# The high part of the gelu of two joint chunks: cast on ScalarE instead of VectorE

## The chip, the cores and the metric

The kernel runs on one core of a Trainium2 chip. The metric is the device time of one execution in microseconds (us); lower is better. Times are medians over runs. The profile comes from one execution of the same program that was taken by the hardware profiler.

## What is computed

Attention with a sliding window and a few global keys (8 heads of 64, 4 batches of 768 rows, a bias that falls with distance), and behind it a two-layer network with an exact gelu. The second half is what the change touches:

```python
def _moe_ref(x, w_in, w_out):        # x: 3072 x 512, w_in: 512 x 2048, w_out: 2048 x 512
    h = x @ w_in
    inv_sqrt2 = np.float32(1.0 / np.sqrt(2.0))
    g = 0.5 * h * (1.0 + erf(h * inv_sqrt2))
    return (g @ w_out).astype(np.float32)

def reference(**kwargs):
    ...
    attn_out = _attn_ref(**attn_kwargs)
    B, H, S, D = attn_out.shape
    x = np.ascontiguousarray(attn_out.transpose(0, 2, 1, 3)).reshape(B * S, H * D)
    return _moe_ref(x=x, **moe_kwargs)
```

## The kernel before

The 3072 rows are cut into 12 chunks of 256 rows, and the hidden width of 2048 into 8 slices of 256. A step is one chunk with one slice: hidden layer (`m1`), gelu (`gelu`), output layer (`m2`). The list STEPS puts the steps in order: step 0 and steps 4 to 18 are the first two chunks with all slices, slice by slice; from step 19 on each later chunk goes through its eight slices.

Products are made in float16 with two parts for each operand: a high part and a low part that holds what the high part left out, so that every product is three matmuls (high with high, high with low, low with high).

The first two chunks are treated jointly from the third slice on (steps 7 to 18, slices 2 to 7): a step then takes one half of a slice for the rows of both chunks, in matmuls of 512 columns (L560), and its output products are those of L698. The 12 gelus of these steps are the ones that the change concerns.

`gelu` works on one 128x512 tile: ScalarE applies Gelu to the hidden layer in PSUM and writes it to SBUF in float32 (gr, L683), VectorE casts it, scaled, to the float16 high part (gh, L684), and VectorE takes the low part (gl, `lo_dve`, L202). Chunks 7 to 11 go another way (`gelu7`), in which ScalarE casts the high parts with activations of kind Copy (L607, L608).

While the first two chunks run, the weights are decoded: each slice comes as four blocks of 64-bit words by DMA on SP's queue (L212); ScalarE converts the low words (L238), VectorE puts the number together in three instructions (L244, L247, L249), ScalarE casts the high part (L259, Copy), and VectorE takes the low part (L202). A word block's buffer is free for the next transfer when its number has been put together.

The attention of the third chunk on (chunk 2 and later) runs beside this: scores on TensorE (L376), masking and maxima on VectorE (L388), exponentials with sums on ScalarE (L419), an addition and a reciprocal of the sums on VectorE (L428, L431), normalization on GpSimd (L437; on VectorE for the first two chunks), transposes on TensorE (L449) with copies on ScalarE (L454), and the products with the values (L488), from which ScalarE casts the high part of x (L539) and VectorE takes the low part (L201).

Exponentials and gelus use different activation tables; a switch shows as ACT_TABLE_LOAD. `table` fixes the order of exponentials and gelus among themselves. Otherwise the order of instructions on each engine is not written out: a planner follows the program's order as a priority and simulates the times, and every engine then takes its queue strictly in that order. `last_dve` (L685) holds the low part of the last gelu; work with low urgency (checks, part of the weight work) is put behind it by `behind`.

Of the kernel before, what the change touches and what calls it, by code (L numbers as in the profile page):

```python
# [13 lines left out]
AF = mybir.ActivationFunctionType  # L14
ALU = mybir.AluOpType
# [30 lines left out]
STEPS = [(c, s) for s in range(NST) for c in range(2)]  # L46
# [11 lines left out]
CAT = 2  # L58
# [4 lines left out]
GS = 2.0 ** 6  # L63
# [42 lines left out]
class Fast:  # L106
# [568 lines left out]
    def gelu(self, t):  # L675
        nc = self.nc
        if STEPS[t][0] >= SEVEN:
            return self.gelu7(t)
        hp = self.h.pop(t)
        gh = self.gp.tile([P, 2, CT], F16, name=f"gh{t}", tag="gh")  # L680
        gl = self.gp.tile([P, 2, CT], F16, name=f"gl{t}", tag="gl")
        gr = self.gp.tile([P, 2, CT], F32, name=f"gr{t}", tag="gr")
        self.table(nc.scalar.activation(out=gr, in_=hp, func=AF.Gelu, scale=1.0 / (WS * XS)))  # L683
        nc.vector.tensor_scalar(out=gh, in0=gr, scalar1=GS, scalar2=None, op0=ALU.mult)  # L684
        self.last_dve = self.lo_dve(gl, gr, gh, GS).ins  # L685
        self.g[t] = (gh, gl)

# [373 lines left out]
```

## Time and profile before

| | |
|---|---|
| median of 3 runs | 639.75 us (638.47 to 641.1) |
| the profiled execution | 639.78 us, of which 638.0 us are the profile's span |
| TensorE matmul busy | 616.9 us (97%) |
| VectorE busy | 485.0 us (76%) |
| ScalarE busy | 387.4 us (61%) |
| GpSimd busy | 83.0 us (13%) |

The profile's times count from the start of the span. PE is TensorE, PEld its weight loads, DVE VectorE, ACT ScalarE, POOL GpSimd, SP the engine that issues most DMAs. A busy time of matmuls is modelled at its end, so neighbouring matmuls overlap in the timeline. Waits are read from semaphore events: the instruction named behind "<-" is the one that came last.

### The profile page before, as it was taken

Reading aid. Unit: us, or ns where it says so; the run is one execution under the profiler, and the core shown is the slowest. Engines: PE = TensorE matmul, PEld = TensorE weight load, DVE = VectorE, ACT = ScalarE, POOL = GpSimd, SP = SyncE. Lnnn points to the kernel's source line nnn. Section 1 sums busy time; section 2 is a strip of 40 time slices with the busy share of each in tenths; the row PEclk is TensorE's granted clock in tenths of the full one; section 3 lists DMA queues with packets and bytes.
Section 4 is the critical chain, followed back from the end, with each engine's and each line's share of the span. In section 5 each row is a group of like instructions: output and inputs, shape, how many; then the busy total and the mean of one; then the engine's idle time right before and its main releaser. Section 6 shows DMA issues by size and latency. Waiting matters only on the chain.

```text
span 638.0 us, 16200 instructions
## 1 busy us (share of the span) xinstructions
PE 616.9 (97%) x6360; PEld 484.2 (76%) x6360; DVE 485.0 (76%) x1482; ACT 387.4 (61%) x891; POOL 83.0 (13%) x175
## 2 busy tenths in 40 slices
PE   7988999999999998999999999999999999999995
PEld 5555544457667887888898888888888888888884
DVE  8979999955777887857867866866856766755875
ACT  3777577754647657657567567576577477574331
POOL 3000006220203112022012022021012021020000
PEclk9988999999999999999999999999999999999999
DMA  8948825304442425143164064043064062000001
GB/s 264 271 167 238 269 96 199 116 1 149 135 131 76 124 64 154 40 145 116 37 173 133 35 174 134 35 150 117 35 174 135 34 174 68 35 1 2 34 2 38
DMA packets 66196, 71.38 MB, mean 112 GB/s; under 512 B 32705, under 2 KB 49345, under 8 KB 66113
## 3 DMA queue, kind: packets, MB, share of 16 engines
q1 hardware_dynamic: 61664, 62.93, 33.0%
q10 hardware_dynamic: 4448, 7.34, 3.2%
q8 instruction: 52, 0.85, 0.6%
q14 instruction: 32, 0.25, 0.1%
HBM read 63.97 MB, written 6.29 MB: 110 GB/s over the span
## 4 chain that ended last, share of the span: by engine, by line
PE 66%; DVE 20%; ACT 8%; issue 3%; DMA 1%; POOL 1%; SPq 0%; POOLq 0%; DVEq 0%; ACTq 0%
PE h L566 27%; PE seven L632 22%; PE av L488 4%; PE s L376 4%; PE t L449 4%; ACT n L419 4%; PE acc L698 2%; PE h L560 2%; DVE ss L606 2%; DVE sf L589 2%; DVE wb L247 1%; DVE wb L249 1%; DVE gl L202 1%; DVE sb L586 1%; DVE wb L244 1%
## 5 line engine op out<-in xcount | busy, mean ns | idle before, releaser
L566 PE MATMUL h<-x,winh 128*128 128x256 f16 x1344 | 227.5, 274 | 4.4 <-DVE mn L388 2.8
L566 PE MATMUL h<-x,winl 128*128 128x256 f16 x672 | 184.2, 274 | 0.0
L566 PEld LDWEIGHTS <-winh 128*128 128x128 f16 x1344 | 128.8, 98 | 24.6 <-DVE mn L388 4.6
L437 POOL TENSOR_SCALAR n<-n,su 128x192 f32<-128x192 f32 (+1 forms) x160 | 77.8, 508 | 483.3 <-DVE su L431 349.1
L601 ACT ACTIVATE gr<-h 128x512 f32<-128x512 f32 x72 | 43.0, 597 | 66.9 <-PE h L566 48.8
L608 ACT ACTIVATE sh<-ss 128x512 f16<-128x512 f32 x72 | 45.4, 630 | 59.6 <-DVE ss L606 59.6
L606 DVE TENSOR_TENSOR ss<-gr 128x128 f32<-128x128 f32 x144 | 37.1, 298 | 55.9 <-ACT gr L601 55.9
L632 PE MATMUL seven<-sw,sh 128*128 128x256 f16 x432 | 74.8, 273 | 0.0
L566 PEld LDWEIGHTS <-winl 128*128 128x128 f16 x672 | 66.0, 98 | 8.4 <-issue 0.5
L419 ACT ACTIVATE n<-n,mn 128x192 f32<-128x192 f32 (+1 forms) x144 | 62.1, 432 | 5.5 <-DVE mn L388 5.4
L632 PEld LDWEIGHTS <-sh 128*128 128x128 f16 x576 | 56.3, 98 | 6.5
L632 PE MATMUL seven<-sw,sl 128*128 128x256 f16 x216 | 58.9, 273 | 0.0
L388 DVE CUSTOM_DVE_ANT_0 n<-s,pens 128x192 f32<-128x192 f32 (+1 forms) x192 | 55.1, 340 | 4.2 <-PE s L376 3.8
L202 DVE SCALAR_TENSOR_TENSOR sl<-ss,sh 128x512 f16<-128x512 f32 x72 | 49.6, 689 | 10.5 <-ACT sh L608 10.5
L202 DVE SCALAR_TENSOR_TENSOR gl<-gr,gh 128x384 f16<-128x384 f32 (+1 forms) x96 | 56.4, 588 | 0.6
L449 PE MATMUL t<-ident,n 128*128 128x128 f32 x288 | 48.0, 277 | 3.2 <-DVE n L437 2.2
L454 ACT COPY pt<-t 128x384 f32<-128x384 f32 x96 | 44.6, 472 | 10.3 <-PE t L449 10.1
L632 PEld LDWEIGHTS <-gh 128*128 128x128 f16 x432 | 41.0, 98 | 9.0 <-issue 4.8
L488 PEld LDWEIGHTS av<-pt,vr 64*64 64x64 f32 (+1 forms) x1312 | 35.9, 135 | 11.8 <-issue 8.3
L376 PE MATMUL s<-kr,qr 64*64 64x192 f32 (+2 forms) x752 | 43.1, 328 | 1.5 <-DMA kr<-kT 1.5
L488 PE MATMUL av<-pt,vr 64*64 64x64 f32 (+2 forms) x1312 | 42.7, 251 | 2.0 <-ACT pt L454 2.0
L449 PEld LDWEIGHTS t<-ident,n 128*128 128x128 f32 x288 | 34.7, 142 | 10.8 <-DVE n L437 2.1
(138 smaller groups left out, 1124.0 us busy)
## 6 DMA issues: line engine op xcount, KB each, us to landing
w<-w SPq DMA_DIRECT2D x32, 512.0 KB, 6.0
c<-w SPq DMA_DIRECT2D x32, 512.0 KB, 4.3
out<-o ACTq DMA_DIRECT2D x23, 256.0 KB, 2.0
qr<-qT SPq DMA_DIRECT2D x11, 512.0 KB, 4.2
vr<-v SPq DMA_DIRECT2D x22, 256.0 KB, 4.4
kr<-kT SPq DMA_DIRECT2D x16, 320.0 KB, 5.5
vr<-v SPq DMA_DIRECT2D x19, 192.0 KB, 3.0
kr<-kT SPq DMA_DIRECT2D x36, 64.0 KB, 3.5
```

Of the source, the lines that this page charges most:

```text
L202: return self.nc.vector.scalar_tensor_tensor(out=out, in0=in_, scalar=scale, in1=hi, op0=ALU.mult, op1=ALU.subtract)
L376: ins = nc.tensor.matmul(out, lhsT=lhs, rhs=rhs, start=True, stop=True).ins
L388: ins = nc.vector.tensor_tensor_reduce(out=nn[:, j * NK:j * NK + n], in0=sp[hh][:, j, 0:n], in1=self.pens[:, 2 * p + hh, o:o + n], scale=- ...
L419: self.table(nc.scalar.activation(out=nn, in_=nn, func=AF.Exp, bias=mn[:, i:i + 1], scale=-1.0, accum_out=su[:, i:i + 1]))
L437: ins = eng.tensor_scalar(out=nn, in0=nn, scalar1=su[:, i:i + 1], scalar2=0.0, op0=ALU.mult, op1=ALU.add)
L449: self.last_t = nc.tensor.transpose(tp[:, i, :], nn[:, o:o + P], self.ident).ins
L454: ins = nc.scalar.copy(pt, tp).ins
L488: ins = nc.tensor.matmul(out, lhsT=lhs, rhs=rhs, start=start, stop=stop, skip_group_check=True).ins
L566: ins = nc.tensor.matmul(hp[:, f, :], lhsT=w[:, d, fs], rhs=x[:, d, e, :], start=n == 0, stop=n == 3 * NP - 1).ins
L606: self.last_sum = nc.vector.tensor_tensor(out=ss[:, o], in0=x, in1=y, op=op).ins
L608: self.last_table = nc.scalar.activation(out=sh, in_=ss, func=AF.Copy, scale=GS).ins
L632: ins = nc.tensor.matmul(out, lhsT=g, rhs=w, start=s == 0 and name in ("P1", "P4", "P6", "P3") and i == 0, stop=s >= NST - 4 and i == 2, s ...
```

## The change

In steps of the first two chunks from the third slice on, the high part of the gelu is made by an activation of kind Copy on ScalarE, with the same scale, instead of the multiplication on VectorE. The other gelus of `gelu`, and all that reads gh, stay as they are.

```diff
@@ -681,7 +681,10 @@
         gl = self.gp.tile([P, 2, CT], F16, name=f"gl{t}", tag="gl")
         gr = self.gp.tile([P, 2, CT], F32, name=f"gr{t}", tag="gr")
         self.table(nc.scalar.activation(out=gr, in_=hp, func=AF.Gelu, scale=1.0 / (WS * XS)))
-        nc.vector.tensor_scalar(out=gh, in0=gr, scalar1=GS, scalar2=None, op0=ALU.mult)
+        if STEPS[t][0] < CAT and STEPS[t][1] > 1:
+            nc.scalar.activation(out=gh, in_=gr, func=AF.Copy, scale=GS)
+        else:
+            nc.vector.tensor_scalar(out=gh, in0=gr, scalar1=GS, scalar2=None, op0=ALU.mult)
         self.last_dve = self.lo_dve(gl, gr, gh, GS).ins
         self.g[t] = (gh, gl)
```

## Rows read from the trace of the kernel before

**Rows 1.** The page, busy time of each engine over the span.
```profile
PE 616.9 (97%) x6360; PEld 484.2 (76%) x6360; DVE 485.0 (76%) x1482; ACT 387.4 (61%) x891; POOL 83.0 (13%) x175
```

**Rows 2.** Windows: start:end, length, busy us of each engine, clock, DMA share, GB/s.
```profile
66.00:150.00 84.00, 82.93 (x554) 41.09 (x552) 72.44 (x182) 55.24 (x124) 17.68 (x24) 1.00 0.40 130
74.00:99.00 25.00, 25.00 (x141) 11.37 (x140) 24.84 (x63) 18.29 (x40) 2.56 (x2) 1.00 0.41 140
99.00:126.00 27.00, 25.93 (x185) 12.45 (x184) 26.70 (x65) 19.13 (x45) 9.43 (x12) 1.00 0.51 167
126.00:150.00 24.00, 24.00 (x188) 13.14 (x187) 12.91 (x40) 13.84 (x34) 5.70 (x12) 1.00 0.09 29
```

**Rows 3.** TensorE's waits, 60 to 155 us: us in total, times, longest.
```profile
PE t L449 <- POOL n L437: 0.8, 1, 0.8
PE h L560 <- DVE x L201: 0.3, 1, 0.3
```

**Rows 4.** TensorE's waits, 205 to 246 us.
```profile
PE h L566 <- DVE mn L388: 2.8, 2, 2.2
```

**Rows 5.** Single lines of the kernel: ns min/median/max, first and last start, forms.
```profile
L684 DVE TENSOR_SCALAR gh<-gr x24: 407/421/573, 41.4 to 197.1; 128x512 f16<-128x512 f32 x24
...
L608 ACT ACTIVATE sh<-ss x72: 625/630/632, 204.6 to 627.8; 128x512 f16<-128x512 f32 x72
```

**Rows 6.** Timeline of VectorE: start, us, engine line operation out<-in.
```profile
90.93 0.41 DVE L684 TENSOR_SCALAR gh<-gr 128x512 f16<-128x512 f32 x1
91.26 0.67 DVE L249 CUSTOM_DVE_ANT_0 wb<-w,wb 128x1024 uint16<-128x1024 uint16 x1
...
94.19 0.15 DVE L428 TENSOR_SCALAR su<-su 128x4 f32<-128x4 f32 x1
...
96.07 0.16 DVE L431 RECIPROCAL su<-su 128x4 f32<-128x4 f32 x1
```

**Rows 7.** The chain of waits in order of time: start, us, what.
```profile
99.35 2.20 POOL n L437 x2
...
101.60 0.44 PE t L449 x2
...
147.06 2.59 PE acc L698 x12
```

**Rows 8.** Timeline of GpSimd, with the idle time before and its releaser.
```profile
96.44 2.93 POOL L437 TENSOR_SCALAR n<-n,su 128x192 f32<-128x192 f32 x2 [90.47 <-DVE su L431]
```

**Rows 9.** Timeline of ScalarE.
```profile
73.80 0.57 ACT L683 ACTIVATE gr<-h 128x512 f32<-128x512 f32 x1
74.28 0.61 ACT L259 ACTIVATE winh<-wb 128x512 f16<-128x512 f32 x1
74.80 0.61 ACT L259 ACTIVATE wouth<-wb 128x512 f16<-128x512 f32 x1
...
88.97 0.60 ACT L683 ACTIVATE gr<-h 128x512 f32<-128x512 f32 x1 [0.40 <-PE h L560]
89.58 1.28 ACT L419 ACT_TABLE_LOAD   x1
...
92.55 0.19 ACT L419 ACTIVATION_READ_ACCUMULATOR n<-n,nmax 128x1 f32 x1
...
114.63 0.60 ACT L683 ACTIVATE gr<-h 128x512 f32<-128x512 f32 x1 [1.77 <-PE h L560]
...
121.36 0.68 ACT L238 ACTIVATE w<-w 128x512 int32<-128x512 uint32 x1 [1.32 <-DMA w<-w]
...
145.59 0.60 ACT L683 ACTIVATE gr<-h 128x512 f32<-128x512 f32 x1
```

**Rows 10.** Timeline of TensorE, first output product of steps 7, 10 and 14.
```profile
79.16 0.38 PE L698 MATMUL acc<-wouth,gh 128*128 128x512 f16 x1
...
94.80 0.38 PE L698 MATMUL acc<-wouth,gh 128*128 128x512 f16 x1
...
119.62 0.39 PE L698 MATMUL acc<-wouth,gh 128*128 128x512 f16 x1
```

## The prediction

> **What bounds the kernel now.** I read the page first. TensorE is busy for 616.9 of 638.0 us [rows 1], so all idle time of TensorE together is 21 us, and only what lies near the change can move. The new casts belong to steps 7 to 18, and the table by windows puts them: between 66 and 150 us TensorE is busy 82.93 of 84.00 us at a granted clock of 1.00, and in 74 to 99 us 25.00 of 25.00 [rows 2]. Busy time is modelled, so I also looked at the pace: twelve 512-column products take 2.59 us [rows 7], 0.22 us each, and that is their distance in the whole stretch. What the stretch has to give is therefore 84.00 - 82.93 = 1.07 us.
>
> VectorE is full there as well: 24.84 of 25.00 us in 74 to 99 and 26.70 of 27.00 in 99 to 126, and it falls to 12.91 of 24.00 after 126 [rows 2]. The chain of waits runs for long parts over VectorE for that reason. It must not be read as "every us taken from VectorE is a us of the kernel", since TensorE is full beside it. The list of TensorE's waits decides: between 66 and 150 us it holds two, 0.8 us of a transpose on GpSimd's normalization and 0.3 us of a hidden-layer product on VectorE's low part of x [rows 3]. These two are the whole 1.07. Later, between 205 and 246 us, there is 2.8 us more, on the masked maxima [rows 4].
>
> **The change part by part.** Removed: 12 casts from VectorE (two chunks, slices 2 to 7). One lasts 0.421 us (median of 24) [rows 5], but the next instruction starts earlier than its end: 90.93 to 91.26 is 0.33 us [rows 6]. So VectorE gets back 12 x 0.33 = 4.0 us, of which eight casts (steps 7 to 14), 2.6 us, lie in its full stretch. The other four lie where it idles for 11.1 of 24.00 us [rows 2].
>
> What those 2.6 us reach is the 0.8 us wait. Going back from the transpose at 101.60, the chain shows two GpSimd operations from 99.35 [rows 7]. They are the last two of four that GpSimd does in one go from 96.44 on, the first two in 2.93 us [rows 8], and the reciprocal on VectorE that releases the first starts at 96.07, 1.88 us after the addition of its sums at 94.19 [rows 6]. The last of these sums is read out on ScalarE at 92.55, ending at 92.74 [rows 9]. So the addition stood in VectorE's queue for 94.19 - 92.74 = 1.45 us after its input was there. Four of the removed casts (the last at 90.93) are ahead of it, and they are worth 4 x 0.33 = 1.3 us. The reciprocal and GpSimd can begin up to 1.3 us earlier, and the transpose too. That is more than the 0.76 us that TensorE stands idle. Against this stands the cast of step 10, now on ScalarE: if it is put ahead of the table load at 89.58 [rows 9], the sums come about 0.52 us later, at 93.26, and the lead is 94.19 - 93.26 = 0.9 us instead of 1.3, still more than 0.76. Gain: 0.76 us. Bounds: 0 (the planner puts other VectorE work into the gap) and 0.76; I take the upper one, since even the smaller lead exceeds the wait.
>
> The 0.3 us wait: VectorE's low part of x follows the cast on ScalarE, which stood behind the conversion of a weight word at 121.36, itself idle for 1.32 us on a transfer [rows 9]. The word's buffer is freed by VectorE, so the transfer may come earlier by up to 2.6 us. Or the chain may grow by the cast of step 14, 0.52 us, on ScalarE ahead of the exponentials that follow the gelu of 114.63. Bounds: 0.27 gained and 0.52 lost, and as 1.32 us of idle time on ScalarE lies between that cast and the place, I take 0.
>
> Added: 12 activations of kind Copy on ScalarE. The nearest row is the same cast of the same size in the later chunks, 0.630 us [rows 5]; successors follow after 0.52 us (74.28 to 74.80) [rows 9]. That is 12 x 0.52 = 6.2 us of ScalarE's queue. Between 74 and 99 us it is busy 18.29 of 25.00 us, then 19.13 of 27.00 and 13.84 of 24.00 [rows 2]; four casts, 2.1 us, come to each, and all three have room for it. No table load is added: the weight cast at 74.28 is a Copy too and follows the gelu of 73.80 directly, with no load between [rows 9].
>
> The way from gelu to its low part: ScalarE can start the cast 0.5 us after the gelu's start and be done 0.63 us later, so 1.13 us after that start. TensorE wants the first of them at 79.16 (gelu at 73.80), the fourth at 94.80 (gelu at 88.97), the eighth at 119.62 (gelu at 114.63) [rows 9, 10]. These leave 4.2, 4.7 and 3.9 us. The tightest is the last: gelu at 145.59 [rows 9], ready at 146.72, wanted at 147.06 [rows 7], a slack of 0.34 us. Cost: nothing, hidden by the matmuls ahead of each; if the cover of the last one is gone, it costs the excess, at most about 0.5 us (one ScalarE instruction put ahead of it).
>
> The added queueing: behind each cast stand exponentials, weight casts, copies of the transposed probabilities and, at the end, casts of x. One place later is 0.52 us for each. In 126 to 150 us ScalarE idles 10 us, so this is absorbed; from the table load at 89.58 on, exponentials stand in a row, and that place I counted above. No DMA moves with the cast; SP's weight transfers wait for VectorE and can only come earlier by the 2.6 us.
>
> After 150 us the chain goes on over gelu, VectorE and ScalarE in turn, with each step released by the one before, so I expect 0.76 us to be kept. Sum: 639.78 - 0.76 = 639.0 us, made against the profiled execution's 639.78, which is beside the median of 639.75.
>
> A rule that speaks against this change: the Trainium skill, page "ScalarE: Activation LUTs", section "Rules for kernel authors", says that multiplications go to VectorE and not to ScalarE, as VectorE is up to about three times as fast per element in bf16. The rows here show the same direction, at a smaller ratio (0.630 against 0.421 us). By that rule the change should lose, as the third rival below works out from the rows.
>
> **The rivals.** First, nothing happens: TensorE is full, the planner (which orders every queue from its own estimate of times, and whose new order no trace shows) fills the gaps of VectorE with weight work, and the reciprocal stays late. For it: VectorE has no idle time before 126 us, so there is always work waiting. Against: the weight work is finite. Time: 639.8.
>
> Second, slower, by a cast that is queued behind a waiting instruction on ScalarE. An engine takes its queue in order; the place is behind the gelu of 114.63, where a table load, exponentials and weight casts follow. If the cast of step 14 is put behind the word conversion that waited until 121.36 for its transfer [rows 9], it starts at 121.36 + 0.52 = 121.9 and ends at 122.5, while TensorE wants it at 119.62 [rows 10]: 2.9 us lost. It decides from the point at which the cast starts later than 119.62 - 0.63 = 119.0. One such case gives 639.0 + 2.9 = 641.9. A second one (step 10 has a table load and the exponentials behind it as well), priced alike for want of a nearer row, makes 644.8. Against it: the cast's input is there 0.5 us after the gelu's start, and a planner that follows readiness would place it at once.
>
> Third, the slower engine counts in full: 12 x (0.630 - 0.421) = 2.5 us if every cast stood on the path, so 642.3. Against it: the 3.9 to 4.7 us of slack at three of the steps above.
>
> Fourth, more than forecast: a new order also removes the 2.8 us of waits at 205 to 246 us [rows 4]. All of both stretches is 1.07 + 2.8 = 3.9 us, so 635.9. Against it: VectorE's work there (sums for the later chunks) isn't touched.
>
> **How the numbers follow.** The forecast (a gain of 0.3 to 1.8 us) gets 0.42; nothing (within 0.3) 0.17; the second rival 0.24, of it 0.13 for two misplaced casts or more; the third 0.04; the fourth, wholly or in part, 0.13. The second gets that much because the new order can't be seen, and an order made from estimated times can be wrong in more than one place. About 0.5%, 3.2 us, is what a measurement can tell from no change, so the bounds are 636.6 and 643.0. Faster by more takes nearly all of the fourth: 0.10. Slower by more takes two misplaced casts and a little of the third: 0.14. Same: 0.76. The range goes from 635.5 (the fourth, and 0.4 for the spread of a measurement) to 642.5 (one misplaced cast or the third, with as much); two misplaced casts are left out.
>
> **What would show it.** In the profile after, 12 casts of 0.63 us on ScalarE and 12 fewer of the 24 on VectorE; GpSimd's first normalization starting about 1 us before 96.44; no wait of a transpose on GpSimd near 101; TensorE idle in 66 to 150 us falling from 1.07 to about 0.3 us. Wrong would be: TensorE waiting for the high part of a gelu on ScalarE (second rival), or a changed idle time after 150 us that outweighs 0.8 us.

## The result and the profile after

The kernel became slower: 645.99 us (median of 9 runs) against 640.92 us (median of 9), a ratio of 1.0081 with a 95% interval of 1.0061 to 1.0101. That is about 5 us against a forecast gain of 0.8 us, and above the end of the range, 642.5.

The page of the profile after has the busy times that the edit must give, and they explain nothing. VectorE falls by 4.2 us and ScalarE rises by 6.4 us, as worked out; TensorE's busy time rises by 4.5 us [rows 1], with the same 6360 matmuls. The three lines are the busy times, TensorE's slices and the granted clock, each digit a fortieth of the span:

```profile
PE 621.4 (96%) x6360; PEld 486.0 (75%) x6360; DVE 480.8 (75%) x1470; ACT 393.8 (61%) x903; POOL 77.8 (12%) x175
...
PE   8987999899999998999999999999999999999995
...
PEclk9898999899999999999999999999999999999999
```

The eighth slice (113 to 129 us) shows both parts of the loss: TensorE is less busy there, and its clock is lower. The table by windows, which answers [rows 2], puts it in 99 to 150 us (start:end, length, then busy us of TensorE, its weight loads, VectorE, ScalarE, GpSimd, granted clock, DMA share, GB/s):

```profile
66.00:150.00 84.00, 81.06 (x487) 38.89 (x485) 66.35 (x167) 58.59 (x129) 12.18 (x23) 0.96 0.38 123
...
99.00:126.00 27.00, 24.06 (x173) 11.75 (x172) 24.28 (x57) 20.14 (x41) 4.15 (x8) 0.94 0.47 163
126.00:150.00 24.00, 24.00 (x134) 11.58 (x133) 9.90 (x41) 15.32 (x39) 5.60 (x13) 0.93 0.03 5
```

In 126 to 150 us TensorE is busy without a pause both times, but it does 134 matmuls where it did 188 [rows 2], some of that because it is later in its work, some because of the clock. TensorE's waits between 60 and 150 us, which answer [rows 3], show where TensorE loses time. The wait on GpSimd is gone, as forecast, the short one on x too, and one that was not there has come:

```profile
PE acc L701 <- ACT gh L685: 2.8, 1, 2.8
PE acc L716 <- DVE gl L202: 1.0, 1, 1.0
```

L685 is the new cast, L701 the output products of the joint steps; the other wait, at 62 us, is in both kernels. ScalarE's queue shows which step it is (timeline: start, us, line, operation, and in brackets the idle time before with what ended it):

```profile
115.93 0.68 ACT L238 ACTIVATE w<-w 128x512 int32<-128x512 uint32 x1
118.69 0.71 ACT L238 ACTIVATE w<-w 128x512 int32<-128x512 uint32 x1 [2.08 <-DMA w<-w]
119.31 0.57 ACT L683 ACTIVATE gr<-h 128x512 f32<-128x512 f32 x1
119.90 1.28 ACT L419 ACT_TABLE_LOAD   x1
...
122.52 0.44 ACT L419 ACTIVATE n<-n,nmax 128x192 f32<-128x192 f32 x1
122.87 0.18 ACT L419 ACTIVATION_READ_ACCUMULATOR n<-n,nmax 128x1 f32 x1
122.96 0.61 ACT L685 ACTIVATE gh<-gr 128x512 f16<-128x512 f32 x1
```

This is step 14. The word conversion (L238, the last block of the last slice) waits 2.08 us for its transfer, the gelu stands behind it, and behind the gelu come a table load and four exponentials before the cast gets its turn. In the kernel before, the same word stood behind the gelu and the exponentials [rows 9]. What TensorE did meanwhile:

```profile
119.88 0.92 PE L376 MATMUL s<-kr,qr 64*64 64x192 f32 x16
123.63 0.61 PE L701 MATMUL acc<-wouth,gh 128*128 128x512 f16 x1 [2.82 <-ACT gh L685]
```

It stood for 2.82 us, and then ran at half the clock. In the windows from 120 us on, the clock is the third column from the end:

```profile
120.80:121.60 0.80, 0.01 (x1) 0.00 (x0) 0.56 (x1) 0.79 (x3) 0.00 (x0) 1.00 0.00 0
121.60:122.40 0.80, 0.00 (x0) 0.00 (x0) 0.00 (x0) 0.80 (x5) 0.00 (x0) 1.00 0.37 31
122.40:123.20 0.80, 0.00 (x0) 0.00 (x0) 0.12 (x2) 0.80 (x5) 0.00 (x0) 0.66 0.76 216
...
126.00:127.00 1.00, 1.00 (x3) 0.30 (x2) 0.89 (x8) 0.91 (x5) 0.61 (x2) 0.50 0.46 80
...
129.00:129.50 0.50, 0.50 (x2) 0.15 (x1) 0.50 (x2) 0.49 (x1) 0.50 (x1) 0.51 0.00 0
129.50:130.00 0.50, 0.50 (x4) 0.23 (x3) 0.29 (x1) 0.50 (x1) 0.50 (x2) 1.00 0.17 33
```

The clock stays at its upper level (2.4 GHz) for the first part of the wait, falls to 0.50 (1.2 GHz) within it and is back at 129.5 us. The chain of waits gives the price: the twelve output products of step 14 take 5.30 us, where twelve at full clock take 2.59 us [rows 7].

```profile
118.69 0.71 ACT w L238
119.40 0.47 ACT gr L683
...
123.05 0.53 ACT gh L685
123.58 0.05 issue
123.63 5.30 PE acc L701 x12
```

The profiles of these kernels differ by up to 1.9 us in their first 60 us, where all do the same work, and again near 245 us, where the clock falls in some and not in others. To compare single profiles I therefore take one distance in each: from the output product that waits 0.97 us at about 62 us (the work ahead of it is that of the kernel before in every run) to the gelu of step 19, the first of the third chunk. Before:

```profile
62.28 0.39 PE L713 MATMUL acc<-wouth,gl 128*128 128x512 f16 x1 [0.97 <-DVE gl L202]
...
152.30 0.60 ACT L683 ACTIVATE gr<-h 128x512 f32<-128x512 f32 x1 [1.24 <-PE h L566]
```

After:

```profile
63.14 0.39 PE L716 MATMUL acc<-wouth,gl 128*128 128x512 f16 x1 [0.97 <-DVE gl L202]
...
158.55 0.60 ACT L683 ACTIVATE gr<-h 128x512 f32<-128x512 f32 x1 [0.92 <-PE h L566]
```

These are 90.02 and 95.41 us: 5.39 us are lost within this stretch, and 5.3 us is still the difference at the last gelu. So hardly anything is lost or won later. Of the 5.39, the wait is 2.82; the twelve products at half clock cost 5.30 - 2.59 = 2.71; the first products of step 15, until the clock is back, some 0.4; and the waits that went gave back 1.0. That makes 4.9, and 0.5 us is left open.

### The profile page after: what moved, and what is told of

It reads as the page before. It is cut to its first block, busy times and chain, and to the rows that moved or that the text cites. A ratio compares the mean times of both kernels' runs of the same rounds, so it can differ in the third digit from the quotient of the medians.

```text
span 644.4 us, 16186 instructions
## 1 busy us (share of the span) xinstructions
PE 621.4 (96%) x6360; PEld 486.0 (75%) x6360; DVE 480.8 (75%) x1470; ACT 393.8 (61%) x903; POOL 77.8 (12%) x175
## 4 chain that ended last, share of the span: by engine, by line
PE 65%; DVE 18%; ACT 11%; issue 3%; DMA 1%; SPq 0%; POOL 0%; POOLq 0%; DVEq 0%; ACTq 0%
PE h L566 27%; PE seven L632 22%; PE av L488 4%; ACT n L419 4%; PE t L449 4%; PE s L376 4%; PE acc L701 2%; PE h L560 2%; DVE ss L606 2%; DVE sf L589 2%; DVE wb L247 1%; DVE sb L586 1%; DVE gl L202 1%; ACT L419 1%; DMA vr<-v 1%
## 5 line engine op out<-in xcount | busy, mean ns | idle before, releaser
L437 POOL TENSOR_SCALAR n<-n,su 128x192 f32<-128x192 f32 (+1 forms) x160 | 72.6, 475 | 494.6 <-DVE su L431 248.7
L608 ACT ACTIVATE sh<-ss 128x512 f16<-128x512 f32 x72 | 45.4, 630 | 59.0 <-DVE ss L606 59.0
L376 PE MATMUL s<-kr,qr 64*64 64x192 f32 (+2 forms) x752 | 44.4, 329 | 0.0
```

Source lines behind the costliest of these rows:

```text
L376: ins = nc.tensor.matmul(out, lhsT=lhs, rhs=rhs, start=True, stop=True).ins
L437: ins = eng.tensor_scalar(out=nn, in0=nn, scalar1=su[:, i:i + 1], scalar2=0.0, op0=ALU.mult, op1=ALU.add)
L608: self.last_table = nc.scalar.activation(out=sh, in_=ss, func=AF.Copy, scale=GS).ins
```

## Experiments

Theory A: the high part of step 14 came late, by its place in ScalarE's queue (behind a word that waits for its transfer, a table load and four exponentials), and the fall of the clock doubled the price. Theory B: a cast on ScalarE is slower and takes 6.2 us of its queue, wherever it stands. Most kernels have one pin (an order that is written out) or one condition. The distance to step 19's gelu is read in each from the same two rows as above, and so from one execution of each kernel; the ratio comes from all runs, and where the two differ, as in the zero products and in "before, word first", the ratio decides. Line numbers shift with the lines that a kernel adds:

| kernel | distance, us | against before | ratio of times (95%) |
|---|---|---|---|
| before | 90.02 | | |
| the change | 95.41 | +5.39 | 1.0081 (1.0061 to 1.0101) |
| casts first | 90.62 | +0.60 | 1.0016 (1.0001 to 1.0031) |
| all but step 14 | 91.67 | +1.65 | 1.0008 (0.999 to 1.0027) |
| only step 14 | 90.23 | +0.21 | 0.9999 (0.9985 to 1.0013) |
| zero products | 94.61 | +4.59 | 1.0050 (1.0031 to 1.0068) |
| word behind the gelu | 93.56 | +3.54 | 1.0060 (1.0047 to 1.0073) |
| before, word first | 94.83 | +4.81 | 1.0039 (1.0025 to 1.0053) |
| both pins | 89.64 | -0.38 | 1.0006 (0.999 to 1.0023) |
| before, word last | 89.98 | -0.04 | 1.0000 (0.9984 to 1.0015) |

**Casts first.** The casts join the order of gelus and exponentials, so that each stands ahead of the next table load:

```diff
-            nc.scalar.activation(out=gh, in_=gr, func=AF.Copy, scale=GS)
+            self.table(nc.scalar.activation(out=gh, in_=gr, func=AF.Copy, scale=GS))
```

> The change, with every cast on ScalarE pinned ahead of the exponentials that follow its gelu. Theory A (the cast of step 14 stood behind a table load and four exponentials, TensorE waited 2.8 us for it and then ran at half the clock for some 5 us): gelu still at about 119.3 us, cast done at 120.5, TensorE wants it at 120.8, so no wait and no drop of the clock; 640 to 641 us, within 0.2% of the kernel before. Theory B (a cast on ScalarE is slower by 0.2 us and its 6.2 us of queue cost, wherever they stand): still 643 to 646 us, ratio above 1.004.

Measured: 641.74 us (12 runs), 0.7 us above the expectation's upper end. All twelve casts are on ScalarE, and of the 5 us about 1 is left (ratio 1.0016, upper end 1.0031, where theory B wanted more than 1.004): theory B falls. Its queue:

```profile
116.71 0.71 ACT L238 ACTIVATE w<-w 128x512 int32<-128x512 uint32 x1 [2.09 <-DMA w<-w]
117.30 0.60 ACT L683 ACTIVATE gr<-h 128x512 f32<-128x512 f32 x1
117.93 0.63 ACT L685 ACTIVATE gh<-gr 128x512 f16<-128x512 f32 x1
118.58 1.28 ACT L419 ACT_TABLE_LOAD   x1
```

The word still waits and the gelu is still late, but the cast is done 0.7 us after it, in time. What is left has a place: TensorE now waits for x, 1.2 us where it was 0.3 [rows 3].

```profile
PE h L560 <- DVE x L201: 1.2, 1, 1.2
```

**All but step 14.** The same planner's order around step 14, word ahead of the gelu, but this one cast on VectorE:

```diff
-        if STEPS[t][0] < CAT and STEPS[t][1] > 1:
+        if STEPS[t][0] < CAT and STEPS[t][1] > 1 and t != 14:
```

> The change in 11 steps; only the cast of step 14 stays on VectorE. ScalarE's order around it is that of the change, the word conversion ahead of the gelu too. Theory A: VectorE casts right behind the gelu of 119.3 us, no wait of TensorE for the high part, clock stays at 1.00; 640 to 641 us. Theory B: eleven twelfths of the 5.1 us remain, about 645.6 us.

Measured: 641.02 us. With this one cast back on VectorE the loss is gone, though the word still stands ahead of the gelu. A wait of TensorE for step 14's parts is left, of 1.0 us and for the low part, and one of 0.7 us for x; the clock stays at 1.00.

```profile
117.50 0.69 ACT L238 ACTIVATE w<-w 128x512 int32<-128x512 uint32 x1 [2.16 <-DMA w<-w]
118.09 0.58 ACT L683 ACTIVATE gr<-h 128x512 f32<-128x512 f32 x1
...
121.10 0.39 PE L701 MATMUL acc<-wouth,gl 128*128 128x512 f16 x1 [0.96 <-DVE gl L202]
```

**Only step 14.**

```diff
-        if STEPS[t][0] < CAT and STEPS[t][1] > 1:
+        if t == 14:
```

> Of the 12 casts only that of step 14 goes to ScalarE. It stands behind the table load and four exponentials as in the change, but the word conversions come behind it, and the gelu comes at 114.6 us as in the kernel before. Theory A (it takes both, the late gelu behind the word and the exponentials ahead of the cast): cast at 118.3 to 118.9 us against 119.6 wanted, no wait; 640 to 641.5 us. Theory C (the place behind the exponentials alone is enough): TensorE waits 2 to 3 us for it and the clock falls; 644 to 646 us.

Measured: 640.91 us, as before. The cast stands behind the table load and the exponentials as in the change, but here the gelu isn't held up:

```profile
113.69 0.60 ACT L683 ACTIVATE gr<-h 128x512 f32<-128x512 f32 x1 [1.80 <-PE h L560]
114.31 1.28 ACT L419 ACT_TABLE_LOAD   x1
117.37 0.62 ACT L685 ACTIVATE gh<-gr 128x512 f16<-128x512 f32 x1
118.41 0.66 ACT L238 ACTIVATE w<-w 128x512 int32<-128x512 uint32 x1
```

TensorE wants the cast at 118.68 here, 0.7 us after it is done. So this cast, moved alone, does no harm: theory C falls. The word comes ahead of the gelu only where the eleven others are moved too. That the planner puts it there because VectorE has room and its own times for the word come earlier is likely, but its times stand in no trace.

**Zero products.** 13 products with a matrix of zeros (wtop, which holds nothing else at this point) are put on TensorE where it waited; they add zero to an accumulator:

```diff
+            if (t, k) == (14, 0):
+                prev = self.last_unit
+                for i in range(13):
+                    ins = nc.tensor.matmul(self.acc[0, 0], lhsT=self.wtop[:, 0, 0:P], rhs=self.xs[:, 0:2, 0, 0, :],
+                                           start=False, stop=False).ins
+                    self.after(ins, prev, "zeros behind the scores")
+                    prev = ins
+                self.zero = prev
...
+                    if t == 14:
+                        self.after(ins, self.zero, "behind the zeros")
```

> The change, with 13 products with a zero matrix (512 columns, 2.8 us at full clock) on TensorE ahead of the output products of step 14, where it waited; they add nothing to the sums. Theory A (the drop of the clock behind the wait costs 2.6 us of its own, 12 products in 5.30 us instead of 2.6): clock stays at 1.00, TensorE has no or hardly any wait, 643 to 643.8 us. Without a share of the clock (the wait is all): 646 us, as the change.

Measured: 644.0 us, 0.2 above the expectation's upper end. The clock is 1.00 in every window from 118 to 126 us: here TensorE, kept busy where it had waited, kept its clock. But the planner also changed the order behind the zeros. The hidden-layer products of the next step (L560) come ahead of step 14's output products (L710 in this kernel; L703 are the zeros), and they wait 1.8 us for x, which the expectation did not have:

```profile
119.74 2.98 PE L703 MATMUL acc<-x,wtop 128*128 128x512 f16 x13
124.50 0.59 PE L560 MATMUL h<-x,winh 128*128 128x512 f16 x2 [1.78 <-DVE x L201]
...
127.09 0.38 PE L710 MATMUL acc<-wouth,gh 128*128 128x512 f16 x1
```

So this kernel differs from the change in more than the clock. It is faster by 0.8 us by the distance and by 2.0 by the medians, and the intervals of the two ratios overlap. That the clock makes products slower is read directly from the change (5.30 us for twelve, against 2.59); what it costs the whole kernel, and whether its 3.1 us simply add to the wait, these runs don't settle.

**Word behind the gelu.** The conversion of the last word (w73 in the code) is pinned behind the gelu of step 14, but stays ahead of the table load:

```diff
+        if t == 14:
+            self.after(self.w73, self.last_table, "the last word behind the gelu")
```

> The change, with only the conversion of the last weight word pinned behind the gelu of step 14. The word still waits for its transfer until about 118.7 us and still stands ahead of the table load, the exponentials and the cast. Theory A (the word, the load and the exponentials ahead of the cast make it late, not the gelu): cast at about 122.4 us, wait of 2.3 us, clock falls; 645 to 646 us. Theory D (the late gelu is what counts): gelu at 115.5 us, no wait, 640 to 641 us.

Measured: 644.81 us, 0.2 under the expectation. The gelu is early, at 115.08, and TensorE still waits 2.5 us for the cast, since word, load and exponentials are all ahead of it. Theory D falls.

```profile
115.08 0.57 ACT L685 ACTIVATE gr<-h 128x512 f32<-128x512 f32 x1
...
121.78 0.61 PE L705 MATMUL acc<-wouth,gh 128*128 128x512 f16 x1 [2.51 <-ACT gh L689]
```

The clock was back sooner (0.50 at 122 to 124 us, 1.00 from 125 on), which fits a smaller loss than the change's.

**Before, word first.** All casts on VectorE; only the order of word and gelu is that of the change:

```diff
+        if t == 14:
+            self.after(self.last_table, self.w73, "the gelu behind the last word")
```

> The kernel before (all casts on VectorE), with the gelu of step 14 pinned behind the conversion of the last weight word, as the planner ordered it in the change. Theory A: what matters is the late high part, whichever engine makes it: the word comes at about 121.4 us, the gelu ends at about 122.5, the cast at 123, TensorE wants it at 119.6; a wait of about 3.4 us and a drop of the clock, 644 to 647 us. If the order of the word costs nothing without the move of the cast: 641 us.

Measured: 644.38 us. With no cast moved at all, the order alone costs 3.2 us by the medians (644.38 against 641.17 in this comparison) and 2.5 by the ratio. The wait came at another place than I wrote:

```profile
PE s L378 <- ACT gr L685: 3.2, 1, 3.2
PE t L451 <- POOL n L439: 0.8, 1, 0.8
```

Scores (L378) wait for the late gelu (L685): they take a PSUM bank (a part of TensorE's result memory) from the pool from which the gelu's input has its own. They do so ahead of the output products. The length (3.2 us against 3.4 expected) and the half clock behind it (0.50 in 122 to 125 us) are as expected. It doesn't contradict "all but step 14", which has the same order and no loss: with all casts on VectorE the transfer of the word ends 3.5 us later (the word starts 120.92 - 61.88 = 59.04 us after the common product, there 117.50 - 61.92 = 55.58), and the gelu with it.

```profile
120.92 0.68 ACT L238 ACTIVATE w<-w 128x512 int32<-128x512 uint32 x1 [1.56 <-DMA w<-w]
121.49 0.60 ACT L685 ACTIVATE gr<-h 128x512 f32<-128x512 f32 x1
```

**Both pins.** The casts first, and the last word behind the casts of x:

```diff
-            nc.scalar.activation(out=gh, in_=gr, func=AF.Copy, scale=GS)
+            self.table(nc.scalar.activation(out=gh, in_=gr, func=AF.Copy, scale=GS))
...
-            nc.scalar.copy(xh, av[j])
+            ins = nc.scalar.copy(xh, av[j]).ins
+            if (c, p, j) == (CAT, 1, 1):
+                self.after(self.w73, ins, "the last word behind the casts of x")
```

> The change with two pins: each cast ahead of the exponentials that follow its gelu, and the conversion of the last weight word behind the casts of x of the third chunk, so that its wait for the transfer holds up neither the gelu of step 14 nor x. Theory A with its completion (the 0.76 us on GpSimd is really gone, and the 1.2 us wait for x that took its place with the casts first comes from the word's wait): no wait of TensorE between 66 and 150 us over 0.3 us, 640.0 to 640.5 us, 0.1 to 0.2% under the kernel before. If the wait for x has another cause: 641 to 642 us as with the casts first.

Measured: 640.88 us against 640.32 of the kernel before in this comparison, no difference that can be told (ratio 1.0006, 0.999 to 1.0023); the 0.1 to 0.2% under the kernel before that I expected do not show. In the trace the idle time is gone, as the forecast had it; between 66 and 150 us:

```profile
66.00:150.00 84.00, 83.95 (x558) 41.76 (x556) 67.61 (x170) 61.80 (x137) 13.45 (x24) 1.00 0.39 131
```

Idle time falls from 1.07 [rows 2] to 0.05 us, but the distance falls by 0.38 only. Where the other 0.6 us went stays open; it isn't idle time of TensorE, and it is of the size that is left open in the change too.

**Before, word last.** The second pin alone, on the kernel before:

> The kernel before with the second pin alone (the last weight word behind the casts of x), all casts on VectorE. It tells what the pin is worth without the move: the 0.3 us wait for x goes, the 0.8 us wait on GpSimd stays; 640.7 us, which can't be told from 641. If this one is as fast as both pins with the move, the casts' move is worth nothing.

Measured: 640.88 us against 640.32, ratio 1.0000. The wait on GpSimd stays at 0.8 us, that for x is 0.2. The expectation's last sentence holds: with no measurable difference between the two, moving these casts is worth nothing that a measurement shows, even where its loss is taken out.

## Why the prediction was wrong

- *TensorE bounds, and only 1.07 us can be won.* Right, as far as the runs tell. In "both pins" 1.02 us of idle time went, and the time did not move measurably; even the forecast's 0.76 us (a ratio of 0.9988) doesn't show there.
- *VectorE gets back 4.0 us, ScalarE takes 6.2 us.* Right: 4.2 and 6.4 us by the page of the profile.
- *The wait on GpSimd goes.* Right in the result, wrong in the way. The reciprocal came at 96.18, which is 0.75 us earlier when the two starts are set against each other (96.18 - 63.14 = 33.04, before 96.07 - 62.28 = 33.79), not 1.3. What went further than I counted is GpSimd itself: its four operations took 2.74 us where they took 5.1 (96.44 to 101.55 [rows 7, 8]).

```profile
96.56 2.74 POOL L437 TENSOR_SCALAR n<-n,su 128x192 f32<-128x192 f32 x4 [90.60 <-ACT w L238]
```

- *"The way from gelu to its low part" costs nothing.* This is the step that failed. Its slack of 3.9 us at step 14 took for granted that the gelu keeps its place and that the cast follows it at once. In the change the gelu starts 56.17 us after the common product (119.31 - 63.14; before, 114.63 - 62.28 = 52.35). That alone leaves 0.4 us: ready at 119.31 + 1.13 = 120.44, wanted at 123.63 - 2.82 = 120.81. And the cast starts 3.65 us after its gelu instead of 0.5 (119.31 to 122.96), which is 3.15 us more. 3.15 - 0.4 = 2.8 us is the wait, measured as 2.82. Neither delay alone exceeds the slack: the late gelu alone ("all but step 14", "casts first") and the late cast alone ("only step 14") cost little or nothing.
- *"SP's weight transfers wait for VectorE and can only come earlier."* Here the gelu's delay was overlooked. They did come earlier: the last word was there at 118.69 (55.55 us after the common product; before, 121.36 and 59.08), by 3.5 us where I had put at most 2.6. I wrote "only", as if earlier could not hurt. But the word now stands ahead of the gelu of step 14 in ScalarE's queue, and its wait for the transfer holds up everything behind. The order of the kernel before, with the word behind the gelu, was no property that the change had to keep.
- *The second rival* named the cast (that of step 14) and the means (a word that waits for its transfer). That its price, 2.9 us, is so near to the 2.82 measured is luck: it has the word behind the gelu and the cast behind the word, at 121.9, while the word came 3.5 us earlier, ahead of the gelu, and a table load and four exponentials made up for it. What it lacked is the clock: a wait of this length was followed by 6 us at half the clock, some 3.1 us more. With it, its case would have given 639.0 + 2.9 + 3.1 = 645.0, if the two simply add. The granted clock stood in the profile, with lower values only in the first 60 us, and I priced no wait with it.
- *The third rival*, the slower engine, is refuted by the casts first. The cast takes 0.630 us there as the nearest row said. The Trainium skill's page "ScalarE: Activation LUTs", section "Rules for kernel authors", gives multiplications to VectorE as the faster engine per element. The trace agrees on the direction (0.630 us on ScalarE, 0.421 on VectorE [rows 5]), but these 0.2 us for each cast are not what the change lost. (L608, from which the 0.630 us come, runs 72 times, 8 for each of nine chunks: ScalarE makes these casts from chunk 3 on, not from chunk 7.)
- *Chances.* I put 0.24 on the second rival and let the forecast rest on a planner that "would place it at once". The order was the one thing that no row showed, and three of my four rivals were on it.

## To carry to other kernels

Work that is taken off a full engine moves more than itself: what that engine fed can come earlier and may slip ahead of urgent work in another in-order queue, and there its own wait is paid by all behind it. After moving an operation, look at what now stands between its input and it, and pin it there (here: ahead of the table load) before judging the move. And when a new wait of a full TensorE is priced, allow for a lower clock behind it too.

## What was not expected of the hardware

The clock's fall depends on more than the length of the wait, as far as these runs show. After waits of 2.82 (the change), 2.5 (word behind the gelu) and 3.2 us (before, word first) it fell; with waits of 1.8 us (zero products) and 1.2 us (casts first) it did not. The wait of 2.2 us on the masked maxima [rows 4] stands in both of the next two profiles with the same idle time, and the clock behind it is 1.00 in the kernel before and 0.83 with the casts first, which may be a part of the spread between runs:

```profile
240.00:250.00 10.00, 7.76 (x80) 6.54 (x79) 8.05 (x33) 7.46 (x21) 1.98 (x5) 1.00 0.76 227
```

```profile
240.00:250.00 10.00, 7.77 (x65) 5.88 (x63) 8.14 (x33) 7.46 (x22) 1.88 (x5) 0.83 0.76 229
```

The second surprise is how much longer GpSimd took beside a busy VectorE: in the kernel before, the first of its four operations took 2.53 us beside a VectorE without a pause, and in the change, where VectorE stood idle for 0.73 us at that time, all four took 2.74 us. This is one observation of each kind, not a test.

```profile
97.08 0.84 DVE L202 SCALAR_TENSOR_TENSOR gl<-gr,gh 128x512 f16<-128x512 f32 x1 [0.73 <-ACT gh L685]
```
